# Attention value blocks of three and two key tiles in place of two, with planned places and one copied score in long cycles

## The chip, the cores and the metric

One core of a Trainium2 chip runs the kernel. The metric is the device time of one execution in microseconds (us), the median of the runs. Engines are called as the profile calls them: PE (TensorE's matmuls), PEld (its weight loads), DVE (VectorE), ACT (ScalarE), POOL (GpSimd), SP (SyncE, which issues the DMAs).

## The reference

```python
x = A_x                                     # 1 x 2048 x 512, float32
xn = _layernorm(x)
q, k, v = split(xn @ wqkv)                  # 32 heads of 16
p = softmax(q @ k.T * 16 ** -0.5)           # full, 2048 keys
s = (p @ v).reshape(B, S, D) @ wo
h = (xn @ w_gate) * (xn @ w_up)             # 1792 wide, no nonlinearity
g = _silu(h @ w_down)
return x + s * g
```

## The kernel before

The attention runs in 32 units: 8 groups of four heads times 4 chunks of 512 queries. A unit has 16 key tiles of 128 keys, and a key tile has four *positions*, one for each head: 2048 positions in all. A position (`position`) issues two things. `expo` multiplies one head's keys of the tile with the chunk's queries into a PSUM bank t (L647), and ScalarE turns it into the exponential tile e (L649), one of `EBUFS` = 11. `score` multiplies queries with 512 keys into a bank s (L625) for a position that lies `LEAD` = 86 further on, and VectorE takes the maximum of each row (L627, `mx`). The maxima of a unit go through four small VectorE operations (`maxima`) and a DMA into two extra rows of the query tile, so that the exponential needs no later correction. Matmuls of t and s use 50 and 48 rows and lie in the lower or upper half of the array; the score of a position takes the other half than its t, so that both run side by side.

A *value block* (`block`, L663, tile `pv`) multiplies the exponentials of some key tiles with V. It uses all 128 rows and 32 columns for each head, so the four heads run side by side; float32 takes two passes per key tile. ScalarE copies the block's sum (`part`, L676) and GpSimd adds it to the unit's sum `acc`. When a unit's blocks are done, `finish` transposes, divides and stores it, in steps of which one runs at a block.

The projections, the feed-forward layer and the output projection are the *filler*: generators `filler` and `ending`, which yield single steps. Nearly all of them are pairs (`pair`): two outputs, whose sums are split over the two halves of the array. A pair has two halves k = 0 and 1 of 12 or 15 steps, each step one lower and one upper matmul (L295, L299). Between the halves the outputs change sides; a ScalarE read of one element (`look`, L303) stands between. When a gate/up pair ends, ScalarE copies g (L411), and VectorE multiplies u with it (L367, in `before_values`, run at the next block); GpSimd splits the product.

The main loop goes cycle by cycle: a number of positions with filler steps between them (not after the first and the last), then one value block of two key tiles. There are 256 cycles. `Filler` deals out each pair over two or three cycles (`spread`, `CYCLES` = 240); where the number is odd, one cycle holds the end of one half and the start of the other, as a tuple. The number of positions in a cycle follows from its steps (`fits`, 7 to 9), and `AHEAD` keeps 1 to 4 positions ahead of the block. The order on PE, ACT, DVE and POOL is the order of the program (`manual_schedule`). PSUM has eight banks: three for t and pv together, three for s, two for the filler's outputs (`misc`).

Ahead of the main loop, `early` does the layer norm, the first projections and V, with the first 86 scores put in at the steps that `EARLY` names. There v tiles are full-array matmuls of 12 steps (`v_proj`, L275). `end` writes the last tiles of the output.

Of the kernel before, what the change touches and what calls it, by code (L numbers as in the profile page):

```python
# [14 lines left out]
OP = mybir.AluOpType  # L15
# [4 lines left out]
P = 128  # L20
# [11 lines left out]
LEAD = 86  # L32
CYCLES = 240
AHEAD = range(1, 5)
SLOTS = 24 * (NC * (NG // 2 - 1) + 1) + 36 * NF * NC
SPLIT_ROUNDS = 3
EBUFS = 11
HBUFS = 2
QBUFS = 2
EARLY = {66: 4, 75: 4, 84: 4, 93: 4, 104: 4, 113: 4, 124: 6, **{142 + 13 * n: 6 for n in range(8)}, 246: 4, 251: 4}  # L40
EARLY_BUFS = {"s": 4, "x": 2, "f": 2}
# [3 lines left out]
ORDER = mybir.DependencyInfo(mybir.DependencyClass.NoSync, mybir.DependencyReason.SCHED_ONLY)  # L45
ORDERED = {mybir.EngineType.PE, mybir.EngineType.Activation, mybir.EngineType.DVE, mybir.EngineType.Pool}


def body(ctx, tc, x, wqkv, wo, wg, wu, wd, out):
# [89 lines left out]

    before_values, behind_values, lighter = [], [], [False]  # L140

# [211 lines left out]
    def v_proj(w, tt, tag):  # L353
        wh, wl = w
        c, t = divmod(tt, 4)
        sl = slice(t * P, (t + 1) * P)
        o = psum(tag, f"v{tt}")
        hi, lo = [lambda d, x=x: x[c][:, d, sl] for x in (xh, xl)]
        yield from full(o, ((hi, lambda d: wh[d]), (hi, lambda d: wl[d]), (lo, lambda d: wh[d])))
        dst = V[:, tt, 0:H * VW].rearrange("p (h e) -> p h e", e=VW)[:, :, 0:DH]  # L360
        nc.scalar.activation(dst, o.rearrange("p (h e) -> p h e", e=DH), AF.Copy)


# [118 lines left out]
    def end(c, t, o, yt, xt):  # L482
        tt = 4 * c + t
        if t == 3 and c == NC - 1:
            for h in range(2):
                part = slice(256 * h, 256 * h + 256)
                nc.vector.tensor_tensor(o[:, part], o[:, part], yt[:, part], op=OP.mult)
                nc.vector.tensor_tensor(yt[:, part], o[:, part], xt[:, part], op=OP.add)
                if h:
                    dma(out[(tt - 2) * P:(tt - 1) * P], fst["y"][:, 1])  # L490
                dma(out[tt * P:(tt + 1) * P, part], yt[:, part])
            return
        nc.vector.tensor_tensor(yt, o, yt, op=OP.mult)
# [17 lines left out]
    def ending():  # L511
# [65 lines left out]
        for t in range(4):  # L577
            final(t)
        for t in range(4):
            end(NC - 1, t, banks[t], fst["y"][:, t], xr[:, t])  # L580
# [34 lines left out]

    def score(n, other, tag="s"):

        i, r = divmod(n, 4 * NT)
        r, j = divmod(r, 4)
        j ^= other  # L620
        kc, t = divmod(r, 4)
        b, pr = 64 * (j % 2), j // 2
        k = ks[(i // NC) % 2]
        o = psum(tag, f"s{i}_{r}_{j}")
        nc.tensor.matmul(o, QS[i][b:b + KB, pr, t * P:(t + 1) * P],  # L625
                         k[b:b + KB, pr, kc * 512:(kc + 1) * 512], start=True, stop=True)
        nc.vector.tensor_reduce(MX[i][:, j, t, kc:kc + 1], o, axis=AX.X, op=OP.max)  # L627

# [23 lines left out]
    def block(todo):  # L652
# [4 lines left out]
        if whole and todo[0][1] == 0:  # L657
            fst["last"] = psum("s", "last")
        o = fst["last"] if whole else psum("st", f"pv{i}")
        for n, (_, kt, es) in enumerate(todo):  # L660
# [18 lines left out]
    def finish(i):  # L679
# [6 lines left out]
        if not late:  # L686
            yield
        if i < NU - 3:
            yield
# [39 lines left out]
    def early():  # L729
# [98 lines left out]
        stream = (n for g in gens for n in g)  # L828
        for n in range(253):
# [44 lines left out]
    class Filler:  # L874
# [6 lines left out]

        def share(self, n, gaps):

            return [n * (i + 1) // gaps - n * i // gaps for i in range(gaps)][::-1]

        def fetch(self):
# [3 lines left out]
            elif v:  # L890
                k, n = v
                self.left = n
                if k == 0:
                    self.whole, odd = divmod(self.cycles(2 * n), 2)
                    self.split = max(2, round(n / (2 * self.whole + 1))) if odd else 0
                    self.more = max(2, self.split - 1) if odd and self.whole else n if odd else 0
                    self.queue = self.share(n - self.split, self.whole) if self.whole else []
                    if odd:
                        self.queue.append((self.split, self.more))
                    if self.whole:  # L900
                        self.queue += self.share(n - self.more, self.whole)

# [8 lines left out]
        def spread(self, gaps):  # L911
            if isinstance(self.now, tuple):
                a, b = self.now
                self.plan = self.share(a, 2) + [0] + self.share(b, gaps - 3)
            else:
                self.plan = self.share(self.now, gaps)

# [8 lines left out]

    cum = [0]

    def spread(n):
        a = cum[0]  # L930
        cum[0] += n
        return max(1, round(cum[0] * CYCLES / SLOTS) - round(a * CYCLES / SLOTS))
# [23 lines left out]

    def position(q):

# [15 lines left out]
        if scored < TOTAL:  # L974
            score(scored, 1)
        step()
# [7 lines left out]
    with tc.manual_schedule(engines=ORDERED):  # L984
        with banks_of(EARLY_BUFS):
            fil = Filler(filler(early()), spread)
        ctx.enter_context(banks_of(BUFS))
        run(fst["v"])
        q = 0
        for b in range(NU * NT // 2):  # L990
            if fil.done:
                parts = iter([3, 2, 2, 2, 2, 2, 2, 2])
                fil = Filler(ending(), lambda n: next(parts))
            work = fil.begin()
            if b >= NU * NT // 2 - 2:
                last = TOTAL - 4 * (NU * NT // 2 - 1 - b)
            else:
# [3 lines left out]
            count = last - q  # L1001
# [9 lines left out]
            if b < NU * NT // 2 - 1:  # L1011
# [5 lines left out]
        block([ready.pop(NU * NT - 2), ready.pop(NU * NT - 1)])  # L1017
        run_all(behind_values)
# [28 lines left out]
```

## Time and profile before

| | |
|---|---|
| median of 3 runs | 1703.11 us (1702.54 to 1703.44) |
| profiled execution | 1702.83 us |
| its span | 1701.0 us |
| PE busy | 1691.5 us, 99% |
| DVE busy | 1434.8 us, 84% |
| ACT busy | 1308.6 us, 77% |
| POOL busy | 875.7 us, 51% |
| granted TensorE clock | 0.999 |

The page gives each engine's busy share and the chain of work that ended last. The timelines give single instructions in order of time; instructions of one line that touch each other are drawn together as one row with their count, so that a gap is read from the start of one row to the start of the next.

### The profile page before, as it was taken

To read this page: it belongs to the slowest core of one execution; us is meant where nothing else is said; L and a number is where in the kernel's file an instruction comes from. 1 tells how busy PE (TensorE), PEld (TensorE's weight loads), DVE (VectorE), ACT (ScalarE), POOL (GpSimd) and SP (SyncE) were. 2 spreads that over 40 slices of the span, in tenths; PEclk is the share of its full clock that TensorE was granted. 3 is DMA by queue.
4 is the path that set the end of the run, shared out by engine and by line. 5 is a ranking of instruction groups with operands and counts; after the bars stand their busy time and mean duration, and the time that the engine had idled before them with its cause. 6 is when DMAs were issued, how large, how long until landed. Compare 5 with 4: busy or idle time off the path is not lost.

```text
span 1701.0 us, 35012 instructions
## 1 busy us (share of the span) xinstructions
PE 1691.5 (99%) x13574; PEld 1037.5 (61%) x13574; DVE 1434.8 (84%) x2485; ACT 1308.6 (77%) x2569; POOL 875.7 (51%) x877
## 2 busy tenths in 40 slices
PE   9999999999999999999999999999999999999998
PEld 6666566566566666656656665666666565665654
DVE  7888888888888888888888888888888888898952
ACT  6367777788777878777877887877778777787774
POOL 5215544753645647446354672663647536455661
PEclk9999999999999999999999999999999999999999
DMA  6217633521241312412015220330225112111362
GB/s 232 88 47 246 221 111 129 142 61 29 60 86 37 116 45 76 82 48 61 29 53 133 72 67 24 88 77 27 58 83 127 55 36 68 32 49 47 116 188 87
DMA packets 117506, 145.92 MB, mean 86 GB/s; under 512 B 12700, under 2 KB 74396, under 8 KB 114652
## 3 DMA queue, kind: packets, MB, share of 16 engines
q1 hardware_dynamic: 117340, 143.69, 29.0%
q8 instruction: 107, 1.75, 0.5%
q14 instruction: 59, 0.48, 0.1%
HBM read 95.94 MB, written 47.45 MB: 84 GB/s over the span
## 4 chain that ended last, share of the span: by engine, by line
PE 98%; DVE 1%; ACT 0%; POOL 0%; DMA 0%; issue 0%; ACTq 0%
PE pv L663 27%; PE t L647 19%; PE s L625 12%; PE y L295 6%; PE u L295 5%; PE g L295 5%; PE g L299 4%; PE u L299 4%; PE y L299 4%; PE v L275 2%; PE p L299 2%; PE p L295 2%; PE z L295 2%; PE last L663 1%; PE z L299 1%; PE p L275 1%
## 5 line engine op out<-in xcount | busy, mean ns | idle before, releaser
L627 DVE TENSOR_REDUCE mx<-s 128x1 f32<-128x512 f32 x2048 | 1255.3, 681 | 209.6 <-PE s L625 170.9
L649 ACT ACTIVATE e<-t 128x512 f32<-128x512 f32 x2048 | 1100.4, 601 | 94.8 <-PE pv L663 39.9
L647 PE MATMUL t<-qs,ks 50*128 50x512 f32 x2048 | 782.3, 407 | 0.0
L625 PE MATMUL s<-ks,qs 48*128 48x512 f32 x2048 | 767.0, 408 | 0.2
L63 POOL TENSOR_TENSOR acc<-acc,part 128x512 f32<-128x512 f32 x214 | 280.1, 1309 | 574.0 <-ACT part L676 573.7
L647 PEld LDWEIGHTS t<-qs,ks 50*128 50x128 f32 x2048 | 359.2, 185 | 268.2 <-issue 109.3
L663 PE MATMUL pv<-e,V 128*32 128x512 f32 x3968 | 477.2, 598 | 0.0
L625 PEld LDWEIGHTS s<-ks,qs 48*128 48x128 f32 x2048 | 350.9, 185 | 26.7 <-issue 4.3
L676 ACT ACTIVATE part<-pv 128x512 f32<-128x512 f32 x214 | 128.0, 598 | 204.2 <-PE pv L663 203.0
L663 PEld LDWEIGHTS pv<-e,V 128*32 128x32 f32 x3968 | 103.7, 109 | 234.9 <-issue 214.9
L299 PE MATMUL g<-fh,w1h 64*128 64x512 f32 x224 | 90.5, 404 | 0.0
L295 PE MATMUL u<-fh,w0h 64*128 64x512 f32 x224 | 90.4, 403 | 0.0
L299 PE MATMUL y<-dh,hh 64*128 64x512 f32 x224 | 89.1, 398 | 0.0
L295 PE MATMUL y<-dh,hh 64*128 64x512 f32 x224 | 89.1, 398 | 0.0
L299 PE MATMUL g<-fl,w1h 64*128 64x512 f32 x224 | 88.1, 393 | 0.0
L299 PE MATMUL u<-fh,w0l 64*128 64x512 f32 x224 | 88.1, 393 | 0.0
L295 PE MATMUL u<-fh,w0l 64*128 64x512 f32 x224 | 88.1, 393 | 0.0
L295 PE MATMUL g<-fl,w1h 64*128 64x512 f32 x224 | 88.0, 393 | 0.0
L299 PE MATMUL u<-fl,w0h 64*128 64x512 f32 x224 | 88.0, 393 | 0.0
L295 PE MATMUL g<-fh,w1h 64*128 64x512 f32 x224 | 87.9, 392 | 0.0
L295 PE MATMUL g<-fh,w1l 64*128 64x512 f32 x224 | 87.9, 392 | 0.0
L299 PE MATMUL g<-fh,w1l 64*128 64x512 f32 x224 | 87.8, 392 | 0.0
(285 smaller groups left out, 2989.1 us busy)
## 6 DMA issues: line engine op xcount, KB each, us to landing
w1r<-in_wg_dram SPq DMA_DIRECT2D x56, 256.0 KB
w0r<-in_wu_dram SPq DMA_DIRECT2D x56, 256.0 KB
wdr<-in_wd_dram SPq DMA_DIRECT2D x56, 256.0 KB
qs<-QD SPq DMA_DIRECT2D x64, 192.0 KB
ks<-KD SPq DMA_DIRECT2D x12, 768.0 KB
KD<-hl SPq DMA_DIRECT2D x16, 512.0 KB
QD<-hl SPq DMA_DIRECT2D x16, 512.0 KB
OD<-acc SPq DMA_DIRECT2D x31, 256.0 KB
```

What stands on the lines that cost most here:

```text
L63: got = getattr(self.engine, name)(*args, **kw)
L275: nc.tensor.matmul(o[:, part], l(d), r(d)[:, part], start=k == d == 0 and not begun, stop=k == 2 and d == ND - 1, skip_group_check=begun)
L295: nc.tensor.matmul(outs[k], l[LOWER], r[LOWER], start=k == 0 and n == 0, stop=(stop or k == 0) and n == len(low) - 1, skip_group_check=k == 1)
L299: nc.tensor.matmul(outs[1 - k], l[UPPER], r[UPPER], start=k == 0 and m == 0, stop=(stop or k == 0) and m == len(high) - 1, skip_group_chec ...
L625: nc.tensor.matmul(o, QS[i][b:b + KB, pr, t * P:(t + 1) * P], k[b:b + KB, pr, kc * 512:(kc + 1) * 512], start=True, stop=True)
L627: nc.vector.tensor_reduce(MX[i][:, j, t, kc:kc + 1], o, axis=AX.X, op=OP.max)
L647: nc.tensor.matmul(o, k[b:b + KR, pr, kt * P:(kt + 1) * P], QS[i][b:b + KR, pr], start=True, stop=True)
L649: nc.scalar.activation(e, o, AF.Exp, scale=DH ** -0.5)
L663: nc.tensor.matmul(o[32 * j:32 * j + 32], V[:, kt, h0:h0 + 32], es[j], start=(kt if whole else n) == 0, stop=kt == NT - 1 if whole else n ...
L676: nc.scalar.activation(part, o, AF.Copy)
```

## The change

The first 4 units have seven value blocks of 2, 3, 2, 2, 3, 2, 2 key tiles, the other 28 have six of 3, 3, 2, 3, 3, 2. `cycles_of` and `parts_of` fix ahead of time how many cycles each pair takes, mostly two with one half each. `plan` chooses the positions of each cycle with a small table of states (positions ahead: 1 to 4 after a block of two, 1 after a block of three), by a cost for positions over `room`. Where a cycle has more positions than `room` and no unit's maxima fall into it, ScalarE copies one score out of PSUM and VectorE's maximum of the copy is issued at the block (`held`). Early v tiles 6 to 13 become pairs and `EARLY` is dealt out anew. After the last scores pv uses a bank of the scores. `finish` has one step less, and `end` does its last product whole.

```diff
-CYCLES = 240
-AHEAD = range(1, 5)
-SLOTS = 24 * (NC * (NG // 2 - 1) + 1) + 36 * NF * NC
+SEVEN, SIX = (2, 3, 2, 2, 3, 2, 2), (3, 3, 2, 3, 3, 2)
+BLOCKS = SEVEN * 4 + SIX * 28
+CYCLES = 184
+HALVES = [3 * ND] * (NC * (NG // 2 - 1) + 1) + NC * [3 * n for third in THIRDS for n in [ND] * len(third) + [len(third)] * 2]
+LAST = [3, 2, 1, 1, 2, 1, 1, 2]
+AHEAD = {2: (1, 4), 3: (1, 1)}
-EARLY = {66: 4, 75: 4, 84: 4, 93: 4, 104: 4, 113: 4, 124: 6, **{142 + 13 * n: 6 for n in range(8)}, 246: 4, 251: 4}
+EARLY = {66: 4, 75: 4, 84: 4, 93: 4, 104: 4, 113: 4, 124: 6, 144: 4, 240: 4, 246: 4,
+         **{144 + 24 * n + m: k for n in range(4) for m, k in ((2, 2), (6, 2), (12, 4), (18, 2), (22, n % 2 * 2))}}
+def shares(n, gaps):
+    return [n * (i + 1) // gaps - n * i // gaps for i in range(gaps)][::-1]
+def cycles_of(k):
+    if k >= len(HALVES):
+        return LAST[k - len(HALVES)]
+    a, b = [round(m * CYCLES / len(HALVES)) for m in (k, k + 1)]
+    return max(1, b - a)
+def parts_of(n, cycles):
+    whole, odd = divmod(cycles, 2)
+    first = max(2, round(n / (2 * whole + 1))) if odd else 0
+    second = max(2, first - 1) if odd and whole else n if odd else 0
+    return ((shares(n - first, whole) if whole else []) + ([(first, second)] if odd else []) +
+            (shares(n - second, whole) if whole else []))
+def room(work):
+    return 2.36 + 0.603 * work
+def plan():
+    work = [w for k, n in enumerate(HALVES + [3 * ND] * len(LAST)) for w in parts_of(n, cycles_of(k))]
+    states, need = {AHEAD[2][1]: (0, [4 * BLOCKS[0] + AHEAD[2][1]])}, 4 * BLOCKS[0]
+    for b, size in enumerate(BLOCKS[1:-1], 1):
+        split = isinstance(work[b], tuple)
+        fits = room(sum(work[b]) if split else work[b]) + split / 2
+        scored = need + LEAD < NG * NC * NT * 4
+        new = {}
+        for ahead, (cost, places) in states.items():
+            for later in range(AHEAD[size][0], AHEAD[size][1] + 1):
+                n = 4 * size + later - ahead
+                c = cost + (max(0, n - fits - 0.5) if scored else 0) + 0.01 * (n - 10) ** 2
+                if n > 3 and (later not in new or c < new[later][0]):
+                    new[later] = c, places + [n]
+        states, need = new, need + 4 * size
+    ahead, (_, places) = min(states.items(), key=lambda s: s[1][0])
+    return places + [4 * BLOCKS[-1] - ahead]
+    def v_pair(w, tts, tag):
+        outs = []
...
+        yield from pair(outs, [(tag, f"v{tt}") for tt in tts], [of(tt) for tt in tts])
+        for tt, o in zip(tts, outs):
+            v_put(tt, o)
-            for h in range(2):
-                nc.vector.tensor_tensor(o[:, part], o[:, part], yt[:, part], op=OP.mult)
-                nc.vector.tensor_tensor(yt[:, part], o[:, part], xt[:, part], op=OP.add)
+            nc.vector.tensor_tensor(yt, o, yt, op=OP.mult)
+            for h in range(2):
+                nc.vector.tensor_tensor(yt[:, part], yt[:, part], xt[:, part], op=OP.add)
-    def score(n, other, tag="s"):
+    def score(n, other, tag="s", copied=False):
+        if copied:
+            kept = part_tile()
+            nc.scalar.activation(kept, o, AF.Copy)
+            held.append(lambda: nc.vector.tensor_reduce(MX[i][:, j, t, kc:kc + 1], kept, axis=AX.X, op=OP.max))
+        else:
+            nc.vector.tensor_reduce(MX[i][:, j, t, kc:kc + 1], o, axis=AX.X, op=OP.max)
-        o = fst["last"] if whole else psum("st", f"pv{i}")
+        o = fst["last"] if whole else psum("s" if late() else "st", f"pv{i}")
         if not late:
-            yield
-        if i < NU - 3:
             yield
-        gens = [k(0), q(0), v(0, 1, 2), k(1), q(1), v(3), k(2), v(4, 5), k(3), v(*range(6, NT - 1))]
+        gens = [k(0), q(0), v(0, 1, 2), k(1), q(1), v(3), k(2), v(4, 5), k(3),
+                *[v_pair(wv, (tt, tt + 1), "fx"[tt // 2 % 2]) for tt in range(6, NT - 2, 2)], v(NT - 2)]
             if isinstance(self.now, tuple):
                 a, b = self.now
-                self.plan = self.share(a, 2) + [0] + self.share(b, gaps - 3)
+                first = (gaps - 1) // 2 if a == b else 2
+                self.plan = shares(a, first) + [0] + shares(b, gaps - 1 - first)
         elif not done:
             step_small(heads)
+        run_all(held)
         run_all(reduced)
         block(rounds)
-        for b in range(NU * NT // 2):
+        for b, (size, count) in enumerate(zip(BLOCKS, plan())):
             work = fil.begin()
-                fits = min(9, max(7, int(2.6 + 0.62 * work))) if q + LEAD < TOTAL and work else 8
-                need = 8 * (b + 1)
-                last = min(max(q + fits, need + AHEAD[0]), need + AHEAD[-1], TOTAL - 4) if b else need + AHEAD[-1]
             fil.spread(max(2, count - 2))
+            unit = (q + count + LEAD) // (4 * NT) > (q + LEAD) // (4 * NT)
+            copied = int(room(work)) - 3 if "pairs" in fst and work > 10 and count > room(work) + 0.2 and not unit else -1
             for k in range(count):
-                position(q)
+                position(q, k == copied)
-                values([ready.pop(2 * b), ready.pop(2 * b + 1)], done)
+            todo = [ready.pop(rounds + n) for n in range(size)]
+            rounds += size
+            if b < len(BLOCKS) - 1:
+                values(todo, done)
```

## Rows read from the trace of the kernel before

**Rows 1.** The page: engines' busy time and the last chain's engines.

```profile
PE 1691.5 (99%) x13574; PEld 1037.5 (61%) x13574; DVE 1434.8 (84%) x2485; ACT 1308.6 (77%) x2569; POOL 875.7 (51%) x877
PE 98%; DVE 1%; ACT 0%; POOL 0%; DMA 0%; issue 0%; ACTq 0%
```

**Rows 2.** PE's timeline around one value block: start us, length us, engine, line, operation.

```profile
805.35 0.39 PE L299 MATMUL u<-fh,w0l 64*128 64x512 f32 x1
805.58 0.40 PE L625 MATMUL s<-ks,qs 48*128 48x512 f32 x1
805.91 1.92 PE L663 MATMUL pv<-e,V 128*32 128x512 f32 x16
807.76 0.50 PE L647 MATMUL t<-qs,ks 50*128 50x512 f32 x1
808.10 0.40 PE L647 MATMUL t<-qs,ks 50*128 50x512 f32 x1
```

**Rows 3.** The weight loads' timeline (PEld) in the same block.

```profile
806.37 0.13 PEld L663 LDWEIGHTS pv<-e,V 128*32 128x32 f32 x4 [0.30 <-issue]
806.79 0.13 PEld L663 LDWEIGHTS pv<-e,V 128*32 128x32 f32 x4 [0.30 <-issue]
```

**Rows 4.** PE's timeline where halves change in mid-cycle, first and last of 42.

```profile
118.50 0.39 PE L647 MATMUL t<-qs,ks 50*128 50x512 f32 x1
118.86 0.49 PE L295 MATMUL p<-fh,w0h 64*128 64x512 f32 x1
119.20 0.39 PE L295 MATMUL p<-fl,w0h 64*128 64x512 f32 x1
...
1602.12 0.50 PE L295 MATMUL z<-fh,w1h 64*128 64x512 f32 x1
```

**Rows 5.** PE's timeline of the first cycle: first t, ninth score, value block.

```profile
95.83 0.50 PE L647 MATMUL t<-qs,ks 50*128 50x512 f32 x1
...
100.21 0.42 PE L625 MATMUL s<-ks,qs 48*128 48x512 f32 x1
...
102.36 1.92 PE L663 MATMUL pv<-e,V 128*32 128x512 f32 x16
```

**Rows 6.** DVE's timeline of the first cycle.

```profile
96.40 7.26 DVE L627 TENSOR_REDUCE mx<-s 128x1 f32<-128x512 f32 x12 [1.84 <-PE t L647]
```

**Rows 7.** ACT's timeline of the first cycle and its block.

```profile
96.49 3.53 ACT L649 ACTIVATE e<-t 128x512 f32<-128x512 f32 x7
...
103.44 0.60 ACT L649 ACTIVATE e<-t 128x512 f32<-128x512 f32 x1 [1.07 <-PE pv L663]
```

**Rows 8.** Groups by line: operations, count, busy us, mean ns, idle before.

```profile
L411 ACT ACTIVATE g<-g 128x512 f32<-128x512 f32 x56 | 33.2, 592 | 0.0
L627 DVE TENSOR_REDUCE mx<-s 128x1 f32<-128x512 f32 x2048 | 1255.3, 681 | 209.6 <-PE s L625 170.9
L636 DVE STREAM_TRANSPOSE mt<-mm 128x32 f32<-128x32 f32 x28 | 5.9, 211 | 1.0
L63 POOL TENSOR_TENSOR acc<-acc,part 128x512 f32<-128x512 f32 x214 | 280.1, 1309 | 574.0 <-ACT part L676 573.7
```

**Rows 9.** PE's timeline in the early v tiles, then that stretch's busy times.

```profile
60.23 0.97 PE L625 MATMUL s<-ks,qs 48*128 48x512 f32 x6
61.13 0.50 PE L275 MATMUL v<-e,xl 128*128 128x512 f32 x1
61.47 2.00 PE L275 MATMUL v<-e,xh 128*128 128x512 f32 x8
...
91.18 1.55 PE L625 MATMUL s<-ks,qs 48*128 48x512 f32 x4
92.66 0.50 PE L275 MATMUL v<-e,xl 128*128 128x512 f32 x1
...
56.20:95.80 39.60, 39.42 (x179) 27.14 (x178) 34.92 (x60) 7.96 (x13) 5.04 (x5) 1.00 0.16 47
```

**Rows 10.** DVE's timeline at the end of the kernel.

```profile
1695.35 0.42 DVE L487 TENSOR_TENSOR z<-z,y 128x256 f32<-128x256 f32 x1
```

More of the change, by code (lines that the diff above doesn't have):

```diff
@@ L138, in step @@
             waiting.pop(0)[1]()
-    before_values, behind_values, lighter = [], [], [False]
+    before_values, behind_values, held, lighter = [], [], [], [False]
     def run_all(queue):
@@ L359, in v_proj, with v_put, of @@
         yield from full(o, ((hi, lambda d: wh[d]), (hi, lambda d: wl[d]), (lo, lambda d: wh[d])))
+        v_put(tt, o)
+    def v_put(tt, o):
         dst = V[:, tt, 0:H * VW].rearrange("p (h e) -> p h e", e=VW)[:, :, 0:DH]
         nc.scalar.activation(dst, o.rearrange("p (h e) -> p h e", e=DH), AF.Copy)
+    def v_pair(w, tts, tag):
+        outs = []
+        wh, wl = w
+        def of(tt):
+            c, t = divmod(tt, 4)
+            sl = slice(t * P, (t + 1) * P)
+            return terms(lambda d: xh[c][:, d, sl], lambda d: xl[c][:, d, sl], lambda d: wh[d], lambda d: wl[d], ND)
+        yield from pair(outs, [(tag, f"v{tt}") for tt in tts], [of(tt) for tt in tts])
+        for tt, o in zip(tts, outs):
+            v_put(tt, o)
     later = []
@@ L578, in ending @@
             final(t)
+        Tied.on, sync.last, pool.last = True, None, None
         for t in range(4):
@@ L626, in score @@
                          k[b:b + KB, pr, kc * 512:(kc + 1) * 512], start=True, stop=True)
-        nc.vector.tensor_reduce(MX[i][:, j, t, kc:kc + 1], o, axis=AX.X, op=OP.max)
+        if copied:
[4 more added lines that the diff above has]
+            nc.vector.tensor_reduce(MX[i][:, j, t, kc:kc + 1], o, axis=AX.X, op=OP.max)
     def maxima(i):
@@ L825, in early @@
         fst["v"] = v_proj(wv, NT - 1, "st")
-        gens = [k(0), q(0), v(0, 1, 2), k(1), q(1), v(3), k(2), v(4, 5), k(3), v(*range(6, NT - 1))]
+        gens = [k(0), q(0), v(0, 1, 2), k(1), q(1), v(3), k(2), v(4, 5), k(3),
+                *[v_pair(wv, (tt, tt + 1), "fx"[tt // 2 % 2]) for tt in range(6, NT - 2, 2)], v(NT - 2)]
         scored = 0
-        stream = (n for g in gens for n in g)
+        stream = (n for g in gens for n in g if n == 1)
         for n in range(253):
@@ L880, in __init__ @@
             self.plan = []
-        def share(self, n, gaps):
-            return [n * (i + 1) // gaps - n * i // gaps for i in range(gaps)][::-1]
         def fetch(self):
@@ L893, in fetch @@
                 if k == 0:
[L894 to L901, printed above, removed]
+                    self.queue = parts_of(n, self.cycles())
         def begin(self):
@@ L913, in spread @@
                 a, b = self.now
-                self.plan = self.share(a, 2) + [0] + self.share(b, gaps - 3)
+                first = (gaps - 1) // 2 if a == b else 2
+                self.plan = shares(a, first) + [0] + shares(b, gaps - 1 - first)
             else:
-                self.plan = self.share(self.now, gaps)
+                self.plan = shares(self.now, gaps)
         def part(self):
@@ L925, in part, with cycles @@
                     self.fetch()
[L927 to L932, printed above, removed]
+    pairs = [0]
+    def cycles():
+        pairs[0] += 1
+        return cycles_of(pairs[0] - 1)
     def values(rounds, done):
@@ L955, in two_finished, with position @@
         return True
-    def position(q):
+    def position(q, copied):
         n, j = divmod(q, 4)
@@ L974, in position @@
         if scored < TOTAL:
-            score(scored, 1)
+            score(scored, 1, copied=copied)
         step()
@@ L985, in body @@
         with banks_of(EARLY_BUFS):
-            fil = Filler(filler(early()), spread)
+            fil = Filler(filler(early()), cycles)
         ctx.enter_context(banks_of(BUFS))
         run(fst["v"])
-        q = 0
-        for b in range(NU * NT // 2):
+        q = rounds = 0
+        for b, (size, count) in enumerate(zip(BLOCKS, plan())):
             if fil.done:
-                parts = iter([3, 2, 2, 2, 2, 2, 2, 2])
-                fil = Filler(ending(), lambda n: next(parts))
+                fil = Filler(ending(), cycles)
             work = fil.begin()
-            if b >= NU * NT // 2 - 2:
-                last = TOTAL - 4 * (NU * NT // 2 - 1 - b)
-            else:
-                fits = min(9, max(7, int(2.6 + 0.62 * work))) if q + LEAD < TOTAL and work else 8
-                need = 8 * (b + 1)
-                last = min(max(q + fits, need + AHEAD[0]), need + AHEAD[-1], TOTAL - 4) if b else need + AHEAD[-1]
-            count = last - q
             fil.spread(max(2, count - 2))
+            unit = (q + count + LEAD) // (4 * NT) > (q + LEAD) // (4 * NT)
+            copied = int(room(work)) - 3 if "pairs" in fst and work > 10 and count > room(work) + 0.2 and not unit else -1
             for k in range(count):
@@ L1010, in body @@
                     fil.part()
-            if b < NU * NT // 2 - 1:
-                values([ready.pop(2 * b), ready.pop(2 * b + 1)], done)
+            todo = [ready.pop(rounds + n) for n in range(size)]
+            rounds += size
+            if b < len(BLOCKS) - 1:
+                values(todo, done)
         run_all(before_values)
@@ L1016, in body @@
             step_small(heads)
-        block([ready.pop(NU * NT - 2), ready.pop(NU * NT - 1)])
+        block(todo)
         run_all(behind_values)
```

## The prediction

> **What bounds the kernel now.** I read the page's busy shares and the chain first: TensorE is busy 99% of the span, and 98% of the chain that ended last is PE [rows 1]. So the time is the sum of what PE issues, and an edit counts if it takes PE time away or makes PE wait. Next I read PE's timeline, because a busy share hides what a change of shape costs. In a cycle, lower-half and upper-half matmuls start in pairs 0.23 us apart (I use 0.2325 over long stretches) [rows 2]. A value block looks different: after the last score 0.33 passes before pv, t starts 1.85 after pv, and the second t 0.34 after the first [rows 2]. The weight loads for the next pass, made as a pass begins, show the second 0.46 after the first and the third 0.42 on [rows 2, 3]; I take 0.43 for each of four, 1.72. So each block costs 0.10 ahead, 0.13 inside and 0.11 behind, **0.34 us beside its arithmetic**. A second loss lies in cycles where a pair changes halves in mid-cycle: 0.36 and 0.34 instead of two slots [rows 4], 0.24 us; I count 42 such cycles, the first and the last standing there.
>
> Third, VectorE. Its reductions follow each other every 0.598 us ((7.26 - 0.68)/11, [rows 6, 8]), and a position with one filler step takes PE only 0.465. PE therefore runs ahead until the three score banks are full. Before does this in one place: its first cycle has 12 positions and 12 steps. Unhindered it is 24 slots, 5.58, with 0.20 for both ends of the block; it takes 6.53 [rows 5], **0.75 us of waiting**. The ninth score, due 4.05 after the first t (0.10 + 17 x 0.2325), starts at 4.38. The law fits the rows: reduction n starts 0.57 + 0.598 n after the cycle begins [rows 5, 6], lasts 0.68, and score n + 3 starts 0.14 after it. That price decides this change.
>
> **The change part by part.** Followed by hand, the new plan gives 196 blocks instead of 256, with the same positions, steps and pv passes.
>
> *Fewer blocks.* 60 x 0.34 = 20.4 us less. The partial sums' ScalarE copies and GpSimd adds also fall by 60; neither is on the chain.
>
> *Half a pair per cycle.* The change of halves moves under a value block, which covers the small ScalarE read that it waits for. Seven cycles still hold a whole pair. 35 x 0.24 = 8.4; I take 8.0.
>
> *Long cycles.* 44 cycles are 12 positions and 12 steps, like that first cycle, but with score 6 copied by ScalarE. Scores 7 and 8 use the banks of scores 4 and 5, which the copy doesn't help, so there the ninth is 0.33 late as in [rows 5]; from there on one reduction less stands in the way and the last score (due 5.45, released at 1.39 + 0.598 x 7 = 5.58, where 1.39 is 0.57 + 0.68 + 0.14; that is inside the delay already paid) adds nothing. Price 0.33 each, with 0.75 as the other end, if the copy brings nothing. No lower end is nearer to nothing than 0.33 unless the first reduction starts earlier than 0.57, which no row shows. 44 x 0.33 = 14.5 us more.
>
> *Ten positions, 12 steps.* The tenth score is due at 4.98 and released at 1.39 + 0.598 x 6 = 4.98: no wait. In 60 such cycles score 6 is copied as well. ScalarE works off exponentials every 0.49 ((3.53 - 0.60)/6, [rows 7]); score 6 ends near 3.82, the copy runs behind that position's exponential from 4.3 to 4.9, and the score that takes the bank may start at 5.04, 0.06 late. Ends 0 and 0.11 (ScalarE 0.05 further behind); 60 x 0.06 = 3.6 more. Cycles of 15 steps (32) come out without a wait by the same law.
>
> *What is queued behind the new wait.* There are 11 e buffers, and a block of three tiles is issued with 13 exponentials outstanding. So two exponentials, not one, wait until pv has read the first tiles: in [rows 5, 7] the waiting one starts 1.08 after pv. It ends at 1.68; the third tile's passes start at about 0.46 + 3 x 0.43 = 1.75, so PE needs it just after. I take 1 us in all, with ends 0 and 0.1 x 128 = 13. Behind the first waiting exponential, ScalarE now also holds the copy of g at the end of a gate/up pair (56 of them, [rows 8]), because it is issued after the last but one position. It ends at 1.08 + 0.49 + 0.6 = 2.17 of a block of 2.71. VectorE's product needs that g, and the held maximum stands behind it: 2.2 + 0.6 + 0.6 = 3.4, while the next reduction would start at 2.71 + 0.57 = 3.28. So about 0.15 late, 0.35 where a unit's four small operations, 0.2 each [rows 8], follow instead of the held maximum. By the plan 28 pair ends fall in three-tile cycles without and 7 with them: 4.2 + 2.4 = 6.6, less what a ten-position cycle can absorb; I take 5.0, ends 0 and 10.
>
> *The early part.* Between the full-array v matmuls every group of scores costs a change of shape: six scores take 0.90 until v instead of three slots, 0.70, and the next v 0.34 [rows 9]: 0.31 each. Of ten groups seven go: 2.2. One group waited 0.8 for its banks (1.48, where four scores need two slots and 0.2, [rows 9]). Against that stand four changes of halves (1.0) and one bank of v14 that its predecessor's copy frees late (0.5), and VectorE was busy 34.9 of 39.6 us there [rows 9], so no more than about 4 can go. I take 2.0 less, ends 4 less and 1 more.
>
> *The tail.* For the last tile two products and two sums of 0.42 us [rows 10] become one whole product, 0.60 by VectorE's pitch, and two sums: 0.3 less. The late cycles and the single step of the finish I cost at nothing: VectorE has no scores left there or has idle time in cycles without a pair end; ends -2 and +2.
>
> Sum: -20.4 - 8.0 - 2.0 - 0.3 + 14.5 + 3.6 + 1.0 + 5.0 = **-6.6 us**. The profiled execution took 1702.83 (span 1701.0, 1.8 around it), 0.3 below the median; against the median 1703.1 this is **1696.5**.
>
> A rule speaks against the change. The Trainium skill, "TensorEngine Tiling (Array Packing)", Performance Considerations, PSUM Bottleneck, says that tiling speeds up TensorE but not the evacuation of PSUM, and that both ScalarE and VectorE should evacuate. This trace agrees with its first half in the 0.75 us of the first cycle; no run so far shows the second half at work. By the rule the 44 long cycles stay bound by VectorE, which is the rival of the next part.
>
> **The rivals.**
> *VectorE becomes the bound (slower).* If ScalarE's copy comes too late to free its bank, a long cycle pays the 0.75 of the first one: 44 x 0.42 = 18.5 more, 1715. It decides from a mean wait of 0.33 + 6.6/44 = 0.48 us per long cycle on: half way between my price and the uncopied one. For it: long cycles follow a block in which g, product and held maximum queue up; against it: ScalarE was 77% busy [rows 1], and while positions are paced by 0.598 it gains on them with its 0.49. Chance 0.25. (The rule of the Trainium skill quoted above would lead here.)
> *It cancels (no change).* The late starts and the e buffers cost their middle (8 and 4 us) and the copied tens 0.11: +3 +3 +3, which leaves 1704 +- 2. For it: every stall lies behind the same queues. Chance 0.25.
> *The waits are smaller (faster by more).* The g copies fall in cycles with slack, no exponential is late, the early part gives all 4: -6.6 - 5 - 1 - 3.6 - 2 = -18, 1685. Against it: the ninth score's 0.33 is measured. Chance 0.14.
> *The change doesn't do what it says:* if a free part buffer keeps ScalarE's copy waiting for GpSimd's add, the copy stalls the exponentials. GpSimd's add sat idle 574 us for ScalarE [rows 8], so the buffer is mostly free in time; I count this in with the first rival.
>
> **How the numbers follow.** The forecast, 1696.5 (own range 1691 to 1701), has 0.36; with the smaller waits, faster by over 0.2% has 0.50. Within 0.2%, about what a measurement of this kernel can tell from no change, has 0.25, slower 0.25. The range takes in half of the smaller-waits case and the slower rival up to two thirds: 1686 to 1711.
>
> **What the profile will show.** Right: 196 blocks; a three-tile block of about 2.71 us with the same 0.34 around it; no mid-cycle change but in seven cycles; long cycles of 8.8 us with a ninth score 0.3 late; first reductions 0.57 after a cycle's start except behind pair ends. Wrong: long cycles over 0.48 us late on average, a gap before the third tile's passes, copies of scores that start a position late, or pv waiting for the exponential whose bank it takes.

## The result: slower by a quarter of a per cent, and the profile after

The changed kernel took **1707.25 us** (median of 11 runs, 1706.23 to 1708.57) against 1702.88 of the kernel before on the same chip: ratio 1.0026, 95% interval [1.0019, 1.0034]. The forecast was 1696.5, faster; the time lies inside its range, on the other side of no change. The profiled execution took 1708.34 (span 1706.6), 5.5 more than that of before.

The page's busy line shows as little as it did in [rows 1]: TensorE at 99%, now of a longer span.

```profile
PE 1695.3 (99%) x13670; PEld 1090.9 (64%) x13670; DVE 1451.2 (85%) x2485; ACT 1316.6 (77%) x2627; POOL 801.0 (47%) x818
PE 97%; DVE 2%; POOL 0%; ACT 0%; issue 0%; DMA 0%; SPq 0%; DVEq 0%; ACTq 0%
```

So I read the timelines cycle by cycle. From a cycle's first matmul to its value block I take off 0.2325 for each slot of two matmuls and 0.2015 for the two ends; what is left is the cycle's *wait*. Added up over PE's timeline of both kernels, up to 1589 us and behind it (by the time at which a cycle's block starts), without the first cycle, which waits 0.75 in both:

| | before | after |
|---|---|---|
| value blocks | 256 | 196 |
| a block of two, of three tiles | 1.855 | 1.855, 2.712 |
| waits up to 1589 us | 15.7 (9.7 of it in the 41 mid-cycle changes of [rows 4] that lie there) | 34.0 |
| of it: 42 cycles of 12 positions and 12 steps | - | 19.9 (0.475 each) |
| of it: 83 cycles of 10 positions and 12 steps | - | 9.1 |
| of it: one wait at 298 us | - | 2.7 |
| waits behind 1589 us | 2.1 | 9.1 |

**A long cycle.** Rows of PE's timeline: the cycle's first t, its ninth score, its last score, the block. Then the block's first weight loads (PEld) with what they waited for, and DVE and ACT of the same cycle, as in [rows 5 to 7].

```profile
311.56 0.49 PE L719 MATMUL t<-qs,ks 50*128 50x512 f32 x1
...
315.93 0.43 PE L692 MATMUL s<-ks,qs 48*128 48x512 f32 x1
...
317.36 0.42 PE L692 MATMUL s<-ks,qs 48*128 48x512 f32 x1
...
317.76 2.78 PE L735 MATMUL pv<-e,V 128*32 128x512 f32 x24
```

```profile
317.76 0.16 PEld L735 LDWEIGHTS pv<-e,V 128*32 128x32 f32 x8 [0.30 <-ACT e L721]
```

```profile
312.13 6.89 DVE L699 TENSOR_REDUCE mx<-s 128x1 f32<-128x512 f32 x11 [0.94 <-PE s L692]
319.96 0.69 DVE L433 TENSOR_TENSOR g<-u,g 128x512 f32<-128x512 f32 x1 [0.95 <-ACT g L477]
320.57 0.68 DVE L697 TENSOR_REDUCE mx<-part 128x1 f32<-128x512 f32 x1
321.16 2.47 DVE L699 TENSOR_REDUCE mx<-s 128x1 f32<-128x512 f32 x4
```

```profile
312.22 3.53 ACT L721 ACTIVATE e<-t 128x512 f32<-128x512 f32 x7
315.56 0.68 ACT L696 ACTIVATE part<-s 128x512 f32<-128x512 f32 x1
316.04 1.67 ACT L721 ACTIVATE e<-t 128x512 f32<-128x512 f32 x3
318.85 0.60 ACT L721 ACTIVATE e<-t 128x512 f32<-128x512 f32 x1 [1.14 <-PE pv L735]
```

The ninth score comes 4.37 after the first t, 0.32 later than its slot: the forecast's 0.33. But the block starts 6.20 after the first t, where the slots give 5.78: 0.42. It starts 0.05 after the tenth exponential has ended (316.04 + 1.67 = 317.71), and its weight load waits for that exponential: pv takes the PSUM bank of the third last t. The same holds in all 111 cycles with a copied score: there the block's first weight load waits for an exponential. So a long cycle has a second limit that the forecast did not have, ScalarE's: first exponential at 0.66, nine more at 0.477, 0.49 for the copy, 0.71 for the tenth itself makes 6.15, and pv at 6.20. The next cycle begins at 320.48, 2.72 after the block, and its first reduction at 321.16, 0.68 after that and not 0.57: product, held maximum and first score queue up on VectorE as forecast. Of the 42 long cycles, 27 start their first reduction at 0.56 or 0.57 and 15 at 0.69 to 0.90; one that starts on time waits 0.42.

The waits by engine and releaser (total us, times, longest) show both queues. Before, the exponential waited for pv 39.9 us in 72 places, and no wait of VectorE for g stood among the longest.

```profile
ACT e L721 <- PE pv L735: 153.7, 120, 2.2
PEld pv L735 <- ACT e L721: 51.5, 173, 0.6
DVE g L433 <- ACT g L477: 41.0, 42, 1.4
```

**The ending.** A late cycle of 12 positions and only 7 steps, on PE (first t, its last two scores, block) and on DVE:

```profile
1602.18 0.50 PE L719 MATMUL t<-qs,ks 50*128 50x512 f32 x1
...
1607.68 0.49 PE L692 MATMUL s<-ks,qs 48*128 48x512 f32 x1
...
1608.28 0.50 PE L692 MATMUL s<-ks,qs 48*128 48x512 f32 x1
1608.70 2.78 PE L735 MATMUL pv<-e,V 128*32 128x512 f32 x24
```

```profile
1602.75 7.27 DVE L699 TENSOR_REDUCE mx<-s 128x1 f32<-128x512 f32 x12 [0.60 <-PE s L692]
```

The scores follow each other at VectorE's 0.60, and the cycle takes 6.52, as long as the first cycle of before took with its 12 steps (6.53, [rows 5]). The slots come to 4.42 and the ends to 0.20: 1.9 us lost in one cycle. Where no scores are left, ScalarE takes VectorE's place. ACT and PE of a cycle with 12 exponentials and 10.5 steps, with the weight load of its last t:

```profile
1654.42 5.00 ACT L721 ACTIVATE e<-t 128x512 f32<-128x512 f32 x10 [1.13 <-PE t L719]
```

```profile
1653.83 0.73 PE L719 MATMUL t<-qs,ks 50*128 50x512 f32 x3
...
1658.99 0.49 PE L719 MATMUL t<-qs,ks 50*128 50x512 f32 x1
1659.41 1.07 PE L735 MATMUL last<-e,V 128*32 128x512 f32 x8
```

```profile
1658.99 0.18 PEld L719 LDWEIGHTS t<-qs,ks 50*128 50x128 f32 x1 [0.20 <-ACT e L721]
```

The block starts 5.58 after the first t; slots and ends make 4.04. Here the block takes no bank of the t, so it waits for no exponential itself. But the t do: from the fourth on they follow each other at ScalarE's pace of about 0.49, the twelfth starts at 1658.99 when the ninth exponential has ended (1658.94), and the block follows 0.42 behind it. From 1589 us to the end the kernel before takes 112.0 us and the kernel after 117.6, with equally many matmuls, 844 (the table by stretch of after):

```profile
1589.00:1706.60 117.60, 110.67 (x844) 66.29 (x840) 63.44 (x108) 76.53 (x153) 38.27 (x39) 0.98 0.38 127
```

**At 298 us** PE's timeline has a hole. The first t of a unit waits for the DMA that brings the maxima; SP's queue shows that DMA behind three loads of weights; the table by stretch shows the granted clock (the column behind POOL) at 0.50 from 300 to 302 us, so at the lower of the two levels, and the block of two tiles takes about 3.2 us instead of 1.855.

```profile
298.15 0.47 PE L719 MATMUL t<-qs,ks 50*128 50x512 f32 x1 [1.98 <-DMA qs<-MD]
...
300.20 3.29 PE L735 MATMUL pv<-e,V 128*32 128x512 f32 x16
```

```profile
289.94 0.64 SPq L114 DMA_DIRECT2D MD<-mt  x1
292.10 0.39 SPq L114 DMA_DIRECT2D w1r<-in_wg_dram  x1
294.03 0.38 SPq L114 DMA_DIRECT2D w0r<-in_wu_dram  x1
294.51 0.45 SPq L114 DMA_DIRECT2D wdr<-in_wd_dram  x1
295.01 1.25 SPq L114 DMA_DIRECT2D qs<-MD  x2
```

```profile
300.00:302.00 2.00, 2.00 (x14) 0.48 (x16) 1.58 (x3) 1.14 (x3) 0.00 (x0) 0.50 0.58 153
```

**The account.** 60 blocks fewer at the forecast's 0.34 are 20.4 us, and the blocks' rows bear it out. Waits: 17.8 before, 43.1 after, 25.3 more. The forecast had for the same things -8.0 + 14.5 + 3.6 + 1.0 + 5.0 = 16.1 more. Of the 9.2 between them 7.0 lie in the ending and 2.7 at 298 us; with the clock there (1.4) and the early part (the first pv stands 0.8 us earlier, not 2.0) that is the 12 us between forecast and profiled execution. And -20.4 + 25.3 + 1.4 - 0.8 makes the 5.5 by which the two profiled executions differ.

### The profile page after: what moved, and what is told of

The parts are those of the page before. It is cut to its first block, busy times and chain, and to the rows that moved or that the text cites. A ratio compares the mean times of both kernels' runs of the same rounds, so it can differ in the third digit from the quotient of the medians.

```text
span 1706.6 us, 35304 instructions
## 1 busy us (share of the span) xinstructions
PE 1695.3 (99%) x13670; PEld 1090.9 (64%) x13670; DVE 1451.2 (85%) x2485; ACT 1316.6 (77%) x2627; POOL 801.0 (47%) x818
## 4 chain that ended last, share of the span: by engine, by line
PE 97%; DVE 2%; POOL 0%; ACT 0%; issue 0%; DMA 0%; SPq 0%; DVEq 0%; ACTq 0%
PE pv L735 27%; PE t L719 18%; PE s L692 13%; PE g L350 6%; PE y L346 5%; PE g L346 5%; PE u L350 4%; PE y L350 4%; PE u L346 4%; PE p L350 2%; PE p L346 2%; DVE mx L699 1%; PE z L350 1%; PE z L346 1%; PE v L326 1%; PE last L735 1%
## 5 line engine op out<-in xcount | busy, mean ns | idle before, releaser
L699 DVE TENSOR_REDUCE mx<-s 128x1 f32<-128x512 f32 x1937 | 1203.0, 684 | 152.1 <-PE s L692 100.3
L692 PE MATMUL s<-ks,qs 48*128 48x512 f32 x2048 | 805.2, 417 | 0.5
L719 PE MATMUL t<-qs,ks 50*128 50x512 f32 x2048 | 793.4, 406 | 2.1 <-DMA qs<-MD 2.0
L114 POOL TENSOR_TENSOR acc<-acc,part 128x512 f32<-128x512 f32 x157 | 205.4, 1308 | 572.9 <-ACT part L748 562.8
L735 PE MATMUL pv<-e,V 128*32 128x512 f32 x3968 | 466.6, 599 | 0.0
L748 ACT ACTIVATE part<-pv 128x512 f32<-128x512 f32 x157 | 93.9, 598 | 110.2 <-PE pv L735 107.6
L346 PE MATMUL u<-fh,w0h 64*128 64x512 f32 x224 | 88.4, 395 | 0.0
L350 PE MATMUL u<-fh,w0h 64*128 64x512 f32 x224 | 88.1, 393 | 0.0
L346 PE MATMUL u<-fh,w0l 64*128 64x512 f32 x224 | 88.0, 393 | 0.0
L350 PE MATMUL y<-dh,hl 64*128 64x512 f32 x224 | 87.9, 393 | 0.0
L346 PE MATMUL g<-fl,w1h 64*128 64x512 f32 x224 | 87.9, 392 | 0.0
```

The source lines that it names most:

```text
L114: got = getattr(self.engine, name)(*args, **kw)
L346: nc.tensor.matmul(outs[k], l[LOWER], r[LOWER], start=k == 0 and n == 0, stop=(stop or k == 0) and n == len(low) - 1, skip_group_check=k == 1)
L350: nc.tensor.matmul(outs[1 - k], l[UPPER], r[UPPER], start=k == 0 and m == 0, stop=(stop or k == 0) and m == len(high) - 1, skip_group_chec ...
L719: nc.tensor.matmul(o, k[b:b + KR, pr, kt * P:(kt + 1) * P], QS[i][b:b + KR, pr], start=True, stop=True)
L735: nc.tensor.matmul(o[32 * j:32 * j + 32], V[:, kt, h0:h0 + 32], es[j], start=(kt if whole else n) == 0, stop=kt == NT - 1 if whole else n ...
L748: nc.scalar.activation(part, o, AF.Copy)
```

## The experiments

**The copy, and where it is needed.** The first kernel makes no copy; the second copies only where a cycle has more than one position over `room`, that is in the cycles of 12 positions and 12 steps.

```diff
-            copied = int(room(work)) - 3 if ... and count > room(work) + 0.2 and not unit else -1
+            copied = -1                                             # the first kernel
+            copied = int(room(work)) - 3 if ... and count > room(work) + 1 and not unit else -1   # the second kernel
```

> The changed kernel, with no score copied by ScalarE. Theory (both queues out of PSUM are near their end, so a copy only shifts waiting from VectorE to ScalarE): the 43 long cycles of 12 positions and 12 steps overrun by 0.95 us as the first cycle of before did, instead of 0.69, so 11 us more; the 59 copied cycles of ten positions and the nine of 12 positions and 15 steps lose 0.11 and 0.14 us less, 7.7 us; the sum is about 1710. Rival one, the copies pay everywhere as they are meant to: the ten-position cycles get longer too and the time is 1718 or more. Rival two, the copies only cost: 1700.

Measured: 1714.12 us (1713.01 to 1715.42), ratio 1.0064 [1.0051, 1.0076]: 6.9 more than after. On average a long cycle waits 0.78 instead of 0.475: twelve reductions again take 7.26 us on DVE, as in [rows 6], the tenth exponential is done 0.6 before the block, and the last score is 0.68 late. So the copy works, about as priced (0.75 without it), and by itself it is worth its place there. My expectation of 1710 was 4 short: without copies the long cycles wait 12.6 more in all and the others 5.8 less (I had 11 and 7.7). In this kernel no block waits for ScalarE but that of the first cycle and two in the ending.

> The changed kernel, with a score copied only in cycles of 12 positions and 12 steps (bound of one position over room instead of 0.2). Theory: a ten-position cycle needs no copy, since its tenth score is due when its bank comes free (4.98 and 4.98 us after the cycle's start), and the copy holds up pv by 0.08 to 0.10 us at its end, as ScalarE comes to the exponential whose bank pv takes that much later. Without it 59 x 0.11 and 9 x 0.14 go: 7.7 us less, about 1699.5. Rival (VectorE starts late in the next cycle, since one reduction more stands behind the cycle's end): no gain, 1707, and first reductions later than 0.57 after a cycle's start.

Measured: 1702.98 us (1701.12 to 1703.48), ratio 0.9995 [0.9986, 1.0004]: 4.3 less than after. Without their copies the ten-position cycles wait 4.8 us in all instead of 9.1, the twelve-position ones with 15 steps 0.6 instead of 1.3. In none of them does the block wait for an exponential any more, where with a copy it does in each. The copies there paid for nothing: the tenth score meets a freed bank anyway, as the forecast's own law said (due 4.98, released 4.98). Its price of 3.6 for the copies in ten-position cycles was near the 4.3 by which their waits fall; the gain from leaving them out is a little over half of the 7.7 that I expected of this run.

**The ending.** Blocks of two tiles and two cycles per pair there, so that no cycle has more positions than its steps cover:

```diff
-BLOCKS = SEVEN * 4 + SIX * 28
+BLOCKS = SEVEN * 4 + SIX * 26 + (2,) * 16
-LAST = [3, 2, 1, 1, 2, 1, 1, 2]
+LAST = [3, 2, 2, 2, 2, 2, 2, 2]
```

> The changed kernel, with value blocks of two key tiles in the last two units, and the last pairs dealt out over the cycles as before (16 blocks instead of 12, 201 cycles for 200 blocks). Theory: nearly all of the loss against before lies behind 1589 us, where the last two units' long cycles have as few as 7 and 8 steps while scores are still due (overruns of 1.1 and 2.1 us), and cycles of 10 to 12 exponentials per block follow: 5 us less, about 1702, with the stretch from 1589 us to the end back at 112 us from 117.6. Rival (the ending waits for the last output tiles' DMAs or the finish step taken away): no gain, 1707.

Measured: 1701.21 us (1700.35 to 1702.70), ratio 0.9988 [0.9979, 0.9997]: 6.0 less than after. The theory holds. VectorE now has seven reductions at a time where it had twelve:

```profile
1598.77 4.27 DVE L699 TENSOR_REDUCE mx<-s 128x1 f32<-128x512 f32 x7
```

**The early part alone**, put into the kernel before (v tiles 6 to 13 as pairs and the new `EARLY`, as in the change's diff):

> The kernel before with the early part of the change alone: v tiles 6 to 13 as pairs, the scores dealt out anew. Theory (VectorE's reductions bound this stretch, so fewer changes of shape give little): the main loop starts 0.8 us earlier, as in the changed kernel, 1702.1. Rival (the forecast's sum of changes of shape, 2.0 us): 1700.9.

Measured: 1702.93 us (1702.49 to 1703.35), ratio 0.9998 [0.9989, 1.0007]. It brings nothing that can be measured; the forecast had 2.0. In its profile the main loop starts 0.95 us earlier than before, but the cycles behind wait 0.9 us more in all.

**The held maximum first.** In `values` the held maximum and a unit's four small operations are issued ahead of VectorE's product:

```diff
     def values(rounds, done):
+        run_all(held)
+        run_all(reduced)
         if before_values:
             run_all(before_values)
         elif not done:
             step_small(heads)
-        run_all(held)
-        run_all(reduced)
         block(rounds)
```

> The kernel after, with the held maximum (and a unit's four small operations) issued ahead of VectorE's product u*g instead of behind it. Theory: in the 42 cycles behind a pair's end VectorE waits up to 0.9 us for ScalarE's g while the held maximum stands behind the product; taken ahead, the held maximum runs during that wait and the next first reduction starts about 0.3 us earlier. Gain 0.1 to 0.15 in some 35 cycles: 4 us, 1703. Rival: the product's wait itself sets the next first reduction (ScalarE's g ends late behind the waiting exponential), or the product's later end holds the filler's bank: 1707. Second rival: the held maximum now makes the product late and so the splits and the next loads: 1709.

Measured: 1703.63 us (1702.97 to 1707.03), ratio 1.0006 [0.9998, 1.0015]: 3.6 less than after. Behind the same long cycle as above VectorE now uses the time in which it waits for g:

```profile
317.02 0.68 DVE L697 TENSOR_REDUCE mx<-part 128x1 f32<-128x512 f32 x1
318.05 0.69 DVE L433 TENSOR_TENSOR g<-u,g 128x512 f32<-128x512 f32 x1 [0.35 <-ACT g L477]
319.12 4.42 DVE L699 TENSOR_REDUCE mx<-s 128x1 f32<-128x512 f32 x7 [0.38 <-PE s L692]
```

That cycle's block starts at 315.85 and lasts 2.71, so the first reduction comes 0.56 after the next cycle's start. VectorE's wait for g falls from 41.0 us to 18.5, the long cycles' waits from 19.9 to 18.2, those of all ten-position cycles from 9.1 to 7.9. All long cycles now start their first reduction at 0.56 or 0.57. The late starts were in the forecast, with 5.0.

**The wait at 298 us.** The first try loads the first gate and up weights earlier:

```diff
-                if m == NG // 2 - 1 and c == NC - 2:
+                if m == NG // 2 - 1 and c == 0:
                     nxt = gu_weights(0)
```

> The kernel after, with the first gate and up weights of the feed-forward layer loaded ten cycles of chunks earlier (at c = 0 of the last projection pair instead of c = NC - 2), so that at the unit boundary at 298 us the DMA of the maxima no longer stands on SP's queue behind three stores that wait for GpSimd. Theory: TensorE's wait of 1.4 to 2.0 us there goes, and with it any time at a low granted clock behind it (0.57 for 3.5 us in the profiled execution of after): 1.5 to 3 us less, 1704.5 to 1705.5, and the times of the runs lie closer together than 1706.2 to 1708.6. Rival: the stores wait on the same splits and the boundary's DMA is late all the same, or the wait is taken up by later waits: 1707.

Measured: 1706.98 us (1706.24 to 1708.11), ratio 1.0022 [1.0013, 1.0032]. A miss, by a wrong reading of mine: the three DMAs ahead of the maxima's are not stores, and not the loads that I moved. They are the loads of the next pair's weights, whose buffers GpSimd's splits free at 292.07 and 294.00 in the profile of after, and they stand in SP's queue as before. The second try ties SP's order to that of the program there (`Tied.on`); it comes last, on top of four edits.

**Four edits together**: copies in long cycles alone, the ending, the held maximum first and the early load of weights.

> The kernel after with four edits: copies of scores in the cycles of twelve positions and twelve steps alone (-4.3 by the run of that edit), blocks of two and two cycles per half in the ending (-6.0 by its run), the held maximum ahead of the product (-4, estimated), the early load of the first gate and up weights (-2, estimated). Theory: these waits lie in different places and their gains add up: 1691, ratio 0.993. Rival: TensorE's waits move to the next queue and half of the gain is lost: 1697 to 1700.

Measured: 1694.34 us (1694.04 to 1696.28), ratio 0.9951 [0.9939, 0.9964]: 12.9 less than after, where 4.3 + 6.0 + 3.6 + 0.3 makes 14.2. The gains nearly add up. The long cycles still wait 19.6 us in all, not 18.2 as with the held maximum first alone: in 21 of the 42 the first exponential now comes 0.72 or more after the cycle's start, not 0.66, where it did so in 6. The kernel with copies in long cycles alone shows the same 21. The 1.4 us are about what is missing from the sum; why the exponential comes later was not tested.

**What ends a long cycle.** Two more kernels, both on the four edits: the score of position 5 is copied instead of 6; then the same with score and copy issued ahead of that position's exponential.

```diff
-            copied = int(room(work)) - 3 if ...
+            copied = int(room(work)) - 4 if ...
@@ position (the second kernel alone)
+        if copied:
+            score(scored, 1, copied=True)
         ready[n][2].append(expo(i, kt, j))
-        if scored < TOTAL:
-            score(scored, 1, copied=copied)
+        if scored < TOTAL and not copied:
+            score(scored, 1)
```

> As the kernel with the four edits, but ScalarE copies the score of position 5 instead of 6 in the long cycles. Theory: the ninth score then takes the bank that ScalarE's copy frees, not one that VectorE's reduction frees; by the law of the pitch 0.598 it is 0.2 late instead of 0.33 (the copy runs behind the exponential of its position, 3.5 to 4.1 us after the cycle's start), and the twelfth 0.13 instead of nothing, within the delay already paid. The exponentials behind the copy also have a position more to catch up before the value block. Gain 0.13 to 0.2 in each of 43 long cycles: 6 to 8 us below the kernel with the four edits, 1684. Rival: the copy frees its bank later than that, and the twelfth score, with one reduction more behind the copy, is as late as the ninth was: the same as the four edits, 1691, or slower by up to 4.

Measured: 1694.70 us (1694.19 to 1696.07), ratio 0.9953 [0.9939, 0.9966]: no gain, where I had expected 6 to 8 us. The long cycles wait 0.47 as before. The copy ends 4.19 after the cycle's start and the ninth score, which now takes its bank, comes at 4.36: as late as when VectorE freed it.

> The kernel with the four edits, but ScalarE copies the score of position 5 and does so ahead of that position's exponential. Theory: a long cycle has two limits that lie within 0.1 us of each other. One is VectorE's: the ninth score 0.33 late. The other is ScalarE's, which the prediction left out: the value block takes the PSUM bank of the third last score tile t, and its exponential, the tenth, ends at 0.66 + 9 x 0.477 + 0.49 for the copy + 0.71 = 6.15 us after the cycle's start; pv starts 0.05 later, at 6.20, where the slots alone would give 5.78. Here the copy frees its bank at 3.9 and the ninth score (due 4.05) no longer waits, so VectorE's limit falls to 0.19; ScalarE still has thirteen pieces of work ahead of the tenth exponential's end, so pv stays at 6.20 to 6.23 and the time at 1694.3 (within 1.5). Rival: the scores alone set the end of a long cycle: 0.13 less in each of 42, 1689.

Measured: 1694.60 us (1694.19 to 1694.74), ratio 0.9948 [0.9934, 0.9962]; the long cycles wait 0.47. The value block stays 0.05 to 0.06 behind the tenth exponential, as ScalarE and PE of the cycle that begins at 309.93 show:

```profile
313.04 0.60 ACT L696 ACTIVATE part<-s 128x512 f32<-128x512 f32 x1
313.53 2.55 ACT L721 ACTIVATE e<-t 128x512 f32<-128x512 f32 x5
```

```profile
314.21 0.46 PE L719 MATMUL t<-qs,ks 50*128 50x512 f32 x1
314.30 0.40 PE L692 MATMUL s<-ks,qs 48*128 48x512 f32 x1
...
316.14 0.64 PE L735 MATMUL pv<-e,V 128*32 128x512 f32 x4
```

The copy is done at 313.64, yet the ninth score starts at 314.30. It comes behind its position's t, and that waits for a bank which the sixth exponential frees, and this one stands behind the copy. ScalarE has thirteen pieces of work ahead of the block in either order, and that sets its start. One part of what I expected did not come: the ninth score did not get earlier. From the ninth t on, every weight load of a t and of the block in this cycle waits for an exponential, so from there ScalarE alone sets the pace. In the order of the change VectorE holds the ninth score, and ScalarE the eleventh and twelfth t and the block. What a cycle would take if ScalarE's share were smaller was not tried.

**SP's order tied** around 298 us, on the four edits:

```diff
-        Tied.on = n < 18
+        Tied.on = n < 18 or 60 <= n < 66
```

> The kernel with the four edits, and SP's order tied to the order of the program from key tile 60 to 65, so that around 298 us the DMA of the maxima stands ahead of the loads of the next gate and up weights (which wait until GpSimd has split the weights before; the run with the early load had moved another pair's loads). Theory: the maxima's DMA is issued when its source has landed, some 3 us earlier, and TensorE's wait of 1.6 us there goes: 1692.5; the times of the runs (1694.0 to 1696.3) lie closer together, because no time at a granted clock of 0.5 to 0.57 follows a wait that is not there. Rival: the loads that now come later make the next pair's split and so TensorE late: 1694 or more.

Measured: **1692.37 us** (1692.19 to 1692.58), ratio 0.9936 [0.9923, 0.9949]: 2.0 less than with the four edits, and 2.2 less than the kernel with the copy ahead (1694.60), which ran on the same chip. PE has no hole there any more, and the runs lie within 0.4 us of each other, those of after within 2.3. SP's queue:

```profile
290.14 0.63 SPq L114 DMA_DIRECT2D MD<-mt  x1
290.88 0.55 SPq L114 DMA_DIRECT2D wdr<-in_wd_dram  x1
292.86 1.26 SPq L114 DMA_DIRECT2D qs<-MD  x2
294.17 0.39 SPq L114 DMA_DIRECT2D w1r<-in_wg_dram  x1
```

The Trainium skill, "DMA: Bandwidth & Descriptors", Anatomy of one DMA — SWDGE (gpsimd) path, says that a wait for a semaphore happens on the issuing sequencer, before the DMA is dispatched. That section describes DMAs on GpSimd's path; the trace agrees for those that SP issues here: with loads in between that wait for their buffers, the maxima's second DMA is issued 5.07 us after the first (295.01 - 289.94), without them 2.72 (292.86 - 290.14).

This version beats both kernels: 10.9 us below the one before, 14.9 below the change.

## Why the prediction was wrong

- **The late cycles, costed at nothing with ends -2 and +2**: this is the step that failed. I gave as reason that VectorE has no scores left there. From 1589 to 1625 us it has: five cycles there wait 3.8 us in all, one of them 1.9. Behind that it has none, and eight cycles wait 5.3 us, 2.8 of it in two whose t go at the pace of ScalarE's exponentials. The law of the first cycle, 6.5 us for 12 reductions however few the steps, and ScalarE's 0.49 were both at hand, and `LAST` and the plan tell how few steps these cycles have. Measured: 7.0 more in the profile, 6.0 by the run that undoes it.
- **A wait that no step had: 298 us.** A DMA that lands too late was among none of the terms. The order of SP's queue puts the loads of a pair, which wait for GpSimd, ahead of the maxima's DMA. Measured: 2.7 of waiting and 1.4 by the clock in the profiled execution, 2.0 in the medians, by the run that ties SP's order.
- **Early part, 2.0**: wrong. Nothing that can be measured; the profile of after shows 0.8. The terms given for it make 2.2 + 0.8 - 1.0 - 0.5 = 1.5, not 2.0.
- **Fewer blocks, 20.4**: right, by the blocks' rows. They take 1.855 and 2.712, and each costs 0.34 beside its arithmetic: 0.2015 at the two ends and 1.855 - 2 x 0.857 = 0.14 inside.
- **Half pairs, 8.0**: borne out by the profiles, with no run of its own. Before's 41 changes in mid-cycle wait 9.7 us up to 1589 us; the two cycles of after that hold a whole pair there wait 0.1.
- **Long cycles, 14.5**: there are 42, not 44. Right in the ninth score (0.32 against 0.33), but short of ScalarE's limit: a long cycle that starts on time waits 0.42, so that limit costs 42 x (0.42 - 0.33) = 3.8. They wait 19.9 in all, of which the run with the held maximum first shows 1.7 to be late starts.
- **Late starts, 5.0**: right in kind, too large. With the held maximum first the waits fall by 1.7 in the long and 1.2 in the ten-position cycles, the time by 3.6.
- **These terms together**: with the half pairs, the ten-position cycles and the late starts the forecast had 16.1 more of waits; measured, without the ending and 298 us, 25.3 - 7.0 - 2.7 = 15.6. That the sum fits is partly luck: a limit that was missing and late starts that were too dear about cancel. Without the ending and 298 us the time would have been about 1707.25 - 6.0 - 2.0 = 1699, near the forecast.
- **The range**: that 1707 lies inside it is luck as well. Its upper part was there for the rival "VectorE becomes the bound", which did not come in the long cycles: its deciding point was 0.48 per long cycle (not half way, which would be 0.54), and it came to 0.475. The rival "it cancels" gives 1696.5 + 9 = 1705.5 by its own terms, not 1704.
- **The waiting exponential, 1.0**: right in kind. The exponential waits for pv in 120 places, and the third tile's passes are not late (blocks of 2.712; there are 120 of them, not 128). What the prediction named among the signs of an error and had no price for is another wait: ahead of the block, pv takes the bank of an exponential not yet done.
- The Trainium skill, "TensorEngine Tiling (Array Packing)", PSUM Bottleneck, wants ScalarE and VectorE both to empty PSUM. Its second half, which no run had shown, holds where VectorE is the limit: the copies in long cycles are worth 11.1 us (the kernel without copies against the one with copies in long cycles alone). Where VectorE is not the limit, the same copy costs: 4.3 us.

## What to carry to other kernels

Here fewer, larger stages saved their fixed cost as counted, and they made the stretches between them longer, so every queue needs a law of its own: VectorE's reductions, ScalarE's exponentials up to the one whose bank comes next, and SP's DMAs. Apply such a law to every stage the plan makes, first to those at the end with little other work to fill them. Relief for one engine that costs another belongs only where the first one is the limit.

## What the runs showed of the hardware

The clock fell behind some of the waits at 298 us, and the length of the wait does not tell which. Behind 1.98 us (profiled execution of after) and 1.68 us (early loads) the granted clock stood at 0.50 (1.2 GHz) from 300 to 302 us. Behind 1.93 us (copy ahead), 1.88 (the ending), 1.82 (copies in long cycles alone) and 1.58 (four edits) it stayed at 1.00. The lower clock would fit that the runs of after lie near 1706.4 and near 1708.1, and those of the last kernel all near 1692.4. The granted clock of whole runs points the same way: with copies in long cycles alone, the six runs of 1702.98 to 1703.48 us had 0.998 and the five of 1701.12 to 1702.16 had 0.999, and 0.001 of the time is 1.7 us. That the clock alone makes the two groups was not shown.
